# First attention of a four-layer kernel: another load order, four moves on the scalar queue, row transposes spread over the attention tiles

## Chip, cores, metric

One core of a Trainium2 chip. The metric is the device time of one execution in microseconds (us). A profile's span, first to last instruction, is about 1.8 us shorter than the time of the same execution. All times below are fast runs, or single profiled runs; those are called looks.

Names used below: TensorE (PE) does the matmuls; VectorE (DVE), ScalarE (ACT) and GpSimd (POOL) do the other arithmetic; transfers (DMA) are issued from the sync, scalar and gpsimd queues, and land when their semaphore shows them complete. An evacuation copies a matmul result out of PSUM, so that its accumulator is free again. A hole is time in which PE stands idle; a half clock is a stretch in which the trace's clock records grant PE 0.5.

## The reference, cut to what matters

Four layers, A B A B, on x of 2048 rows by 576. A is an attention of 32 heads of 18, each row looking at 8 rows at a distance of two. B is a gated layer. Row normalisation and residual additions, which matter here only as work between the layers, are cut.

```python
qkv = x @ wqkv                               # A: q, k, v of 576 each
logits = einsum('bhsd,bhswd->bhsw', q, kg) * scale   # 8 rows a head, masked
o = einsum('bhsw,bhswd->bhsd', softmax(logits), vg)
A = o.reshape(B, S, D) @ wo
# ...
z = gelu(einsum('bsd,df->bsf', x, w_in))     # B: its first half is gated by
                                             # a product over rows of the second
```

## The kernel before: the parts concerned

Everything below is in the first layer. Projections of q and k leave PSUM for staging tiles (`stg`, and `win2a`, lent for the last two head groups), and small transfers ("moves") carry 18-row pieces to their place in `QK`, from which the logits are computed. Eight moves belong to the last group, d = 4.

```python
def PG(d, qk, cc, dve, queues=(nc.sync, nc.gpsimd)):
    # ... five matmuls, evac() into stg; when a staging tile is full:
    for dst, src in moves:
        dma_rr[0] += 1
        self.dma(dst, src, eng=queues[dma_rr[0] % len(queues)])

def VW(t, hh, dve):                     # one v group: five matmuls into pv, then
    # ...
    evac(v_ext[...], pv[...], dve)      # VectorE if dve, else ScalarE

q2 = (nc.gpsimd, nc.sync, nc.gpsimd)
# ... loads, all on the sync queue
self.load_wv(nc.sync, 2)
x_load(x1[:, 0:4, :], 4, 4, nc.sync)    # x rows 512 on
self.load_wqk(nc.sync)                  # k, q, rest of k
# ... projections
PG(d, qk, cc, False, (nc.gpsimd, nc.sync) if d in (0, 4) else q2)
# ...
T_(12, 13, 14, 15)                      # row transposes of x rows 1536 on (sync queue)
for t in range(nvw0, nvw - (1 if li == 0 else 0)):
    for hh in range(2):
        VW(t, hh, li == 0)
```

The attention then runs in half tiles ("steps") of a table. Row transposes of the new x, which the gated layer needs, are put at steps:

```python
at(s + 2, LN_XN, i)                     # normalised row tile i; tiles 4 to 12 into stg
if i < NS - 1:
    at(max(s + 4, 24 + (5 * i) // 4) if li == 0 else s + 4, LN_T, i)   # its transpose
```

Every plain transposing transfer stands on the sync queue: the row transposes (`xnT`) and those of the attention output (`oT`). The gated layer's big tile `Z` is laid by the program over memory that the first attention used, `stg` included.

The softmax here doesn't subtract the row's maximum and nothing guards it: scores larger than these inputs give would overflow.

Of the kernel before, what the change touches and what calls it, by code (L numbers as in the profile page):

```python
# [19 lines left out]
D = 576  # L20
# [42 lines left out]
class K:  # L63
# [219 lines left out]
        nc.vector.memset(R["wv"][64:128, 4, :], 0.0)  # L283
        nc.vector.memset(R["wo"][64:128, 4, :], 0.0)

    def load_wqk(self, eng):

        R = self.right
        for c0, n, w0 in ((D, 512, D + 64), (0, D, 0), (D + 512, 64, D)):
            self.dma(R["wqk"][:, :, w0:w0 + n], self.A_wqkv[0:512, c0:c0 + n].rearrange("(c p) n -> p c n", p=P), eng=eng)  # L290
            self.dma(R["wqk4"][:64, w0:w0 + n], self.A_wqkv[512:576, c0:c0 + n], eng=eng)

# [29 lines left out]
    def layer_A(self, li):  # L322
        nc, tc, cfg = self.nc, self.tc, self.cfg
# [9 lines left out]
        NSTG, CBW = (3 if li == 0 else 4), 1024  # L333
        stgs = [main.tile([P, 2, CBW], bf16, name=f"stg{k_}") for k_ in range(NSTG)]
# [20 lines left out]
        def tdim(t):  # L355
            nq = min(QT, S - QT * t)
            return HALO + nq, nq
# [11 lines left out]
        def evac(out, in_, dve):  # L369
            if dve:  # L370
                nc.vector.tensor_copy(out=out, in_=in_)  # L371
            else:
                nc.scalar.copy(out=out, in_=in_)

        def VW(t, hh, dve):
            nk = tdim(t)[0]
            pv = self.PT_tile([P, 512], f32, "pv")
            for c in range(5):
                nc.tensor.matmul(pv[:nk, 0:288], lhsT=self.xnT[:, c, QT * t:QT * t + nk],  # L379
                                 rhs=wv_sb[:, c, hh * 288:(hh + 1) * 288], start=(c == 0), stop=(c == 4))  # L380
            evac(v_ext[:nk, t, 16 * hh:16 * hh + 16, 0:DH], pv[:nk, 0:288].rearrange("p (b d) -> p b d", d=DH), dve)
# [4 lines left out]
        def PG(d, qk, cc, dve, queues=(nc.sync, nc.gpsimd)):  # L386

            cb, gi = divmod(cc, CBW // 512)
            key = (d, cb)
            if key not in stg_tiles:  # L390
                if cb == 0 and d >= 3 and lent:
                    stg_tiles[key] = lent[d - 3]
                else:
                    stg_tiles[key] = stgs[stg_rr[0] % NSTG]
                    stg_rr[0] += 1
                stg_left[key] = (2 if d < 4 else 1) * (CBW // 512)
            stg = stg_tiles[key]
            pp = self.PT_tile([P, 512], f32, "pp")
            w0 = d * P + (640 if qk else 0)
            for c in range(5):  # L400
                w = wqk[:, c, w0:w0 + P] if c < 4 else wqk4[:, w0:w0 + P]
                nc.tensor.matmul(pp[:, :], lhsT=w, rhs=self.xnT[:, c, PADL + cc * 512:PADL + (cc + 1) * 512],  # L402
                                 start=(c == 0), stop=(c == 4))
            evac(stg[:, qk, gi * 512:(gi + 1) * 512], pp[:, :], dve)
            stg_left[key] -= 1
            if stg_left[key] == 0:
                stg_tiles.pop(key)
                cs = slice(PADL + cb * CBW, PADL + (cb + 1) * CBW)
                moves = []
                for h in range(d * P // DH, H):  # L410
                    a, b = max(h * DH, d * P), min((h + 1) * DH, (d + 1) * P)
                    if a >= b:
                        break
                    g, rg = divmod(h, 4)
                    q0, s0, n = 32 * rg + a - h * DH, a - d * P, b - a
                    if d < 4:
                        moves.append((QK[q0:q0 + n, :, g, cs], stg[s0:s0 + n, :, :]))
                    else:
                        for a_ in range(2):
                            moves.append((QK[q0:q0 + n, a_, g, cs], stg[64 * a_ + s0:64 * a_ + s0 + n, 0, :]))  # L420
# [3 lines that stand above are left out]
# [81 lines left out]
        def LN_XN(i):  # L505
            mv, rstd, nmr = tails[i].pop("ln")
            xn = None
            if li == 0 and 4 <= i < 4 + 3 * NSTG:
                k_, m = divmod(i - 4, 3)
                xn = stgs[(2 + k_) % NSTG][:].rearrange("p a b -> p (a b)")[:, 640 * m:640 * (m + 1)]  # L510
            tails[i]["xn"] = self.ln_xn(tails[i]["x"], P, mv, rstd, nmr, eng="pool", xn=xn)

        def LN_T(i):
# [2 lines left out]
        q2 = (nc.gpsimd, nc.sync, nc.gpsimd)  # L516


        if li == 0:
# [3 lines left out]
            def x_load(xg, i0, n, eng):  # L523
                self.dma(xg, self.A_x[i0 * P:(i0 + n) * P, :].rearrange("(i p) d -> p i d", p=P), eng=eng)
                for k_ in range(n):
                    xts[i0 + k_] = xg[:, k_, :]
# [3 lines left out]
            x_load(x0[:, 1:2, :], 1, 1, nc.scalar)  # L530
            x_load(x0[:, 2:4, :], 2, 2, nc.sync)
            self.load_wv(nc.sync, 2)
            x_load(x1[:, 0:4, :], 4, 4, nc.sync)
            self.load_wqk(nc.sync)
            x_load(spare, 8, 4, nc.sync)
            exp_table()
            self.zero_right()
# [12 lines left out]
            def S_(*tiles):  # L550
                for i in tiles:
                    st = sb.tile([P, 2, nc.vector.BN_STATS_DIM], f32, name="ln_st", tag="ln_st", bufs=3)
                    for s in range(2):
                        nc.vector.bn_stats(out=st[:, s, :], in_=xts[i][:, s * 288:(s + 1) * 288])
                    nc.vector.bn_aggr(out=mvs[:, i, :], in_=st[:])

            def R_(i0, n):
                rs = rstds[:, i0:i0 + n]
                nc.vector.tensor_scalar_add(out=rs, in0=mvs[:, i0:i0 + n, 1], scalar1=EPS)
                nc.gpsimd.tensor_tensor(out=rs, in0=rs, in1=self.neg_half[:, 0:1].to_broadcast([P, n]), op=ALU.pow)  # L560
# [29 lines left out]
            VW(0, 0, False)  # L590
            VW(0, 1, False)
            VW(1, 0, False)
            S_(3)
            R_(2, 2)
            rows[1]()
# [2 lines left out]
            A_(2, 3)  # L598
            T_pe(2)
            T_pe(3)  # L600
            VW(1, 1, False)
            x_load(sb.tile([P, 4, D], bf16, name="x_in3", tag="x_in", bufs=2)[:], 12, 4, nc.sync)
            S_(4, 5)
            R_(4, 2)
# [18 lines left out]
            order = [(d, 0) for d in range(4)] + [(d, 1) for d in range(4)] + [(4, 0), (4, 1)]  # L623
            for k_, (d, cc) in enumerate(order):
                for qk in ((1, 0) if d < 4 else (0,)):
                    PG(d, qk, cc, False, (nc.gpsimd, nc.sync) if d in (0, 4) else q2)
                if k_ == 3:
                    VW(3, 0, False)
                    VW(3, 1, False)
                if k_ == 5:  # L630
                    R_(12, 4)
                    A_(12, 13, 14, 15)
            T_(12, 13, 14, 15)
            nvw0, nvw = 4, 9
        else:
# [12 lines left out]
            nvw0, nvw = 0, 4  # L648
        for t in range(nvw0, nvw - (1 if li == 0 else 0)):
            for hh in range(2):  # L650
                VW(t, hh, li == 0)

        pieces = []

# [8 lines left out]
        def at(s, f, *a):  # L663
            table.setdefault(s, []).append((f, a))
# [6 lines left out]
        for t in range(nvw, NT):  # L671
            for hh in range(2):
                if li == 0 and t == nvw:
                    at(13 * hh, VW, t, hh, True)
                else:
                    at(2 * t - 2 + hh, VW, t, hh, 2 * t - 2 + hh >= PG_END and hh == 0)
        for i in range(NS):
            t = -(-(i + 1) * P // QT) - 1
            s = 2 * t + (6 if li == 0 and t < 10 else 5 if t < NT - 5 else 4 if t < NT - 3 else 3)
            at(s - 5, XO, i)  # L680
            at(s, WO, i, 0)
            at(s + 1, WO, i, 1)
            at(s + 1, LN_STATS, i)
            at(s + 2, LN_XN, i)
            at(s + 2, XST, i)
            if i < NS - 1:
                at(max(s + 4, 24 + (5 * i) // 4) if li == 0 else s + 4, LN_T, i)
        if li == 0:
            at(0, self.load_wo, nc.sync)
            for f in reversed(self.load_win2a(nc.gpsimd)):  # L690
                at(0, f)
        at(PG_END + 2, alloc_win2b)
        for k_ in range(6):
            at(PG_END + 2 + 2 * k_, win2b_piece, k_)
# [9 lines left out]
        if li == 0:  # L704
            VW(nvw - 1, 0, False)
            VW(nvw - 1, 1, False)
        for s in range(NST):
            if s + 1 < NST:
                L_mm(s + 1)
                EXP(s + 1)  # L710
            PV(s)
            for f, a in table.pop(s, []):
                f(*a)
# [339 lines left out]
```

## Time and profile before

| | |
|---|---|
| median of 3 runs | 1192.48 us (1191.74 to 1193.84) |
| span and mean granted clock of the profiled run | 1190.8 us, 0.998 |
| TensorE (PE) busy | 99% of the span |
| first logits; end of the attention's last output projection | 41.31 us; 135.31 us |

PE is the bound; only its holes, and stretches in which its clock is halved, can be won or added. The prediction shows the page's first lines and the waits. Two more views matter for what follows. First PE's timeline of the kernel before (start, length in us, line, operation, tiles, count, and in brackets the idle time before with what ended it):

```profile
34.05 5.16 PE L379 MATMUL pv<-wv_sb,xnT 128*128 128x288 bf16 x40
39.05 2.32 PE L402 MATMUL pp<-xnT,wqk_sb 128*128 128x512 bf16 x10
41.31 0.40 PE L437 MATMUL L_ps<-QK 32*128 32x112 bf16 x16
```

No bracket: eight v groups run on end, then two projections, then the first logits. Now the sync queue in the same view:

```profile
28.38 7.74 SPq L77 DMA_DIRECT2D QK<-stg  x9
...
41.93 5.20 SPq L249 DMA_TRANSPOSE xnT<-ln_xn  x4
```

Nine and seven moves are issued without a break (7.74 and 5.61 us, 0.8 us each), and then the four transposes of x rows 1536 on, which landed by 50.02 us. The attention loop's first projection needs them.

### The profile page before, as it was taken

To read this page: it belongs to the slowest core of one execution; us is meant where nothing else is said; L and a number is where in the kernel's file an instruction comes from. 1 tells how busy PE (TensorE), PEld (TensorE's weight loads), DVE (VectorE), ACT (ScalarE), POOL (GpSimd) and SP (SyncE) were. 2 spreads that over 40 slices of the span, in tenths; PEclk is the share of its full clock that TensorE was granted. 3 is DMA by queue.
4 is the path that set the end of the run, shared out by engine and by line. 5 is a ranking of instruction groups with operands and counts; after the bars stand their busy time and mean duration, and the time that the engine had idled before them with its cause. 6 is when DMAs were issued, how large, how long until landed. Compare 5 with 4: busy or idle time off the path is not lost.

```text
span 1190.8 us, 20761 instructions
## 1 busy us (share of the span) xinstructions
PE 1180.2 (99%) x8554; PEld 620.6 (52%) x8554; DVE 547.4 (46%) x1206; ACT 376.6 (32%) x593; POOL 281.5 (24%) x383
## 2 busy tenths in 40 slices
PE   8999999999999999999999999999999999999998
PEld 5567544444444444457755775444444444444677
DVE  8688587333233233245556786753233233233311
ACT  5578677210110110202156786760110110111000
POOL 4768685000000000001153877530000000000000
PEclk9999999999999999999999999999999999999999
DMA  8989992000000000049645999900000000000332
GB/s 195 200 163 199 181 224 65 23 4 9 12 12 12 12 1 11 12 139 291 169 98 117 203 227 196 202 14 9 12 12 1 12 12 12 12 1 28 125 105 73
DMA packets 178104, 101.21 MB, mean 85 GB/s; under 512 B 134336, under 2 KB 159360, under 8 KB 178009
## 3 DMA queue, kind: packets, MB, share of 16 engines
q1 hardware_dynamic: 165144, 78.13, 30.6%
q0 software_dynamic: 6512, 16.00, 5.4%
q10 hardware_dynamic: 6352, 5.75, 1.6%
q8 instruction: 67, 1.10, 0.4%
q14 instruction: 29, 0.23, 0.1%
HBM read 42.39 MB, written 16.53 MB: 49 GB/s over the span
## 4 chain that ended last, share of the span: by engine, by line
PE 94%; DMA 3%; POOL 1%; ACT 0%; issue 0%; SPq 0%; DVE 0%; ACTq 0%; DVEq 0%
PE pg L887 42%; PE pz L869 12%; PE po L941 12%; PE pz L791 11%; PE pp L402 5%; PE pw L494 3%; PE O_ps L457 3%; PE pv L379 3%; PE L_ps L437 2%; DMA oT<-o_t 2%; PE pzs L791 1%; DMA QK<-win2a 1%; POOL QK L77 1%; DMA wqk_sb<-in_A_wqkv_dram 1%; ACT P_sb L446 0%
## 5 line engine op out<-in xcount | busy, mean ns | idle before, releaser
L887 PE MATMUL pg<-Wq,Z 128*128 128x512 bf16 x2304 | 502.8, 379 | 0.0
L887 PEld LDWEIGHTS <-Z 128*128 128x128 bf16 x2304 | 225.3, 98 | 272.0
L891 DVE TENSOR_TENSOR g_tmp<-pg,ln_xn 128x512 f32<-128x512 f32 x144 | 99.6, 692 | 429.2 <-PE pg L887 429.2
L881 ACT ACTIVATE z1T<-pz 128x1024 bf16<-128x1024 f32 x72 | 73.7, 1024 | 513.8 <-PE pz L869 513.6
L77 POOL DMA_DIRECT2D wout<-in_B_w_out_dram x4 | 4.3, 1064 | 604.6 <-PE pg L887 604.6
L941 PE MATMUL po<-wout,Z 128*128 128x288 bf16 x1152 | 141.4, 286 | 0.0
L446 ACT ACTIVATE P_sb<-L_ps 128x896 bf16<-128x896 f32 (+1 forms) x152 | 126.7, 887 | 41.2 <-PE L_ps L437 40.6
L869 PE MATMUL pz<-xnT,w 128*128 128x512 bf16 (+1 forms) x640 | 136.0, 380 | 0.0
L941 PEld LDWEIGHTS <-Z 128*128 128x128 bf16 x1152 | 112.7, 98 | 28.8
L791 PEld LDWEIGHTS <-xnT 128*128 128x128 bf16 (+1 forms) x800 | 66.2, 97 | 81.0 <-issue 23.7
L791 PE MATMUL pz<-win2a,xnT 128*128 128x512 bf16 x384 | 104.8, 380 | 0.0
L892 DVE TENSOR_TENSOR Z<-g_tmp,z1T 128x512 bf16<-128x512 f32 x144 | 99.6, 692 | 9.7
L869 PEld LDWEIGHTS <-w 128*128 128x128 bf16 (+1 forms) x640 | 51.1, 97 | 80.0 <-issue 27.1
L402 PE MATMUL pp<-xnT,wqk_sb 128*128 128x512 bf16 x360 | 83.8, 382 | 0.5 <-DMA wqk_sb<-in_A_wqkv_dram 0.5
L805 ACT ACTIVATE zp<-pz 128x1024 bf16<-128x1024 f32 x64 | 65.5, 1024 | 36.6 <-PE pz L791 32.8
L951 DVE TENSOR_TENSOR x_new<-po,xo 128x288 f32<-128x288 f32 (+1 forms) x64 | 28.8, 455 | 87.6 <-PE po L941 83.5
L791 PE MATMUL pz<-win2b,xnT 128*128 128x512 bf16 (+1 forms) x256 | 65.7, 380 | 0.0
L807 DVE CUSTOM_DVE_ANT_0 Z<-zp 128x1536 bf16<-128x1536 bf16 x32 | 56.6, 1769 | 13.1 <-ACT zp L805 13.0
L77 POOL DMA_DIRECT2D QK<-stg x81 | 50.7, 631 | 36.3 <-DVE stg L371 21.0
L379 PE MATMUL pv<-wv_sb,xnT 128*128 128x288 bf16 (+1 forms) x380 | 55.8, 285 | 0.0
L242 POOL TENSOR_SCALAR ln_xn<-x_new,ln_mv,ln_rstd 128x576 bf16<-128x576 f32 x23 | 52.8, 2294 | 2.0
L402 PEld LDWEIGHTS <-wqk_sb 128*128 128x128 bf16 x360 | 33.2, 98 | 37.2 <-DMA wqk_sb<-in_A_wqkv_dram 1.0
(114 smaller groups left out, 916.9 us busy)
## 6 DMA issues: line engine op xcount, KB each, us to landing
xres<-x_new SPq DMA_DIRECT2D x48, 288.0 KB
xo<-xres SPq DMA_DIRECT2D x32, 288.0 KB
wout<-in_B_w_out_dram POOLq DMA_DIRECT2D x4, 1296.0 KB, 8.5
xo<-xres SPq DMA_DIRECT2D x8, 576.0 KB
w<-in_B_w_in_dram SPq DMA_DIRECT2D x16, 256.0 KB
QK<-stg POOLq DMA_DIRECT2D x53, 72.0 KB, 4.4
QK<-stg SPq DMA_DIRECT2D x41, 72.0 KB
xo<-in_A_x_dram SPq DMA_DIRECT2D x8, 288.0 KB
```

Of the source, the lines that this page charges most:

```text
L77: return eng.dma_start(out=out, in_=in_)
L379: nc.tensor.matmul(pv[:nk, 0:288], lhsT=self.xnT[:, c, QT * t:QT * t + nk], rhs=wv_sb[:, c, hh * 288:(hh + 1) * 288], start=(c == 0), stop ...
L402: nc.tensor.matmul(pp[:, :], lhsT=w, rhs=self.xnT[:, c, PADL + cc * 512:PADL + (cc + 1) * 512], start=(c == 0), stop=(c == 4))
L446: nc.scalar.activation(out=P_bufs[(2 * s + jp) % 4][:nk, :, :, 0:nq], in_=Lv[:nk, :, :, 0:nq], func=ACT.Exp, scale=scale)
L791: nc.tensor.matmul(pzvs[ci][:, sub * 512:sub * 512 + w], lhsT=self.xnT[r0:r1, c, PADL + i * P:PADL + (i + 1) * P], rhs=win2(c)[r0:r1, c0 + ...
L805: nc.scalar.activation(out=zp[:, c0:c0 + cn], in_=pzvs[ci][:, 0:cn], func=ACT.Gelu_apprx_tanh, accum_out=sums[:, ci:ci + 1])
L869: nc.tensor.matmul(pz1s[q // 2][:, q % 2, :], lhsT=w1[r0:r1, c, sub * P:(sub + 1) * P], rhs=self.xnT[r0:r1, c, PADL + q * 512:PADL + (q + ...
L881: nc.scalar.activation(out=z1T[:, q2 * 512:(q2 + 2) * 512], in_=pz1s[q2 // 2][:, :, :].rearrange("p a b -> p (a b)"), func=ACT.Gelu_apprx_ ...
L887: nc.tensor.matmul(pg[:, :], lhsT=Z[:, jj, i, sub * P:(sub + 1) * P], rhs=Wq[q][:, i, :], start=(i == 0), stop=(i == NS - 1))
L891: nc.vector.tensor_tensor(out=tmp[:], in0=pg[:, :], in1=bsp[:, qs], op=ALU.add)
L892: nc.vector.tensor_tensor(out=uT(jj)[:, sub, qs], in0=tmp[:], in1=z1Ts[jj, sub][:, qs], op=ALU.mult)
L941: nc.tensor.matmul(acc[hh], lhsT=uT(j // 2)[:, j % 2, i * P:(i + 1) * P], rhs=wouts[j // NJH][:, j % NJH, hh * 288:(hh + 1) * 288], start= ...
```

## The change

Its intent: q weights sooner; the gpsimd queue, whose last moves landed late, relieved by the scalar queue, with VectorE relieved of four v evacuations; and the sync queue free for output transposes.

```diff
-            x_load(x1[:, 0:4, :], 4, 4, nc.sync)
-            self.load_wqk(nc.sync)
+            self.load_wqk(nc.sync, ("k", "q0"))      # q0: the first 256 columns of q
+            x_load(x1[:, 0:4, :], 4, 4, nc.sync)
+            self.load_wqk(nc.sync, ("q1", "k1"))
...
-                    PG(d, qk, cc, False, (nc.gpsimd, nc.sync) if d in (0, 4) else q2)
+                    PG(d, qk, cc, False, (nc.gpsimd, nc.sync) if d == 0 else q2 if d < 4 else (nc.scalar, nc.sync))
...
-                VW(t, hh, li == 0)
+                VW(t, hh, li == 0 and t > 5)         # v tiles 4 and 5 now on ScalarE
...
-                at(max(s + 4, 24 + (5 * i) // 4) if li == 0 else s + 4, LN_T, i)
+                at(s + 4 if li > 0 or i > 12 else 21 + 2 * i if i < 7 else 35 + (i - 7) // 2, LN_T, i)
...
+            VW(nvw, 0, False)                        # taken out of step 13, ahead of the loop
```

Cut: one v group earlier in the prologue, another staging tile for the first normalised rows, and the order of six later weight loads.

More of the change, by code (lines that the diff above doesn't have):

```diff
@@ L284, in zero_right, with load_wqk @@
         nc.vector.memset(R["wo"][64:128, 4, :], 0.0)
-    def load_wqk(self, eng):
+    def load_wqk(self, eng, names=("k", "q", "k1")):
         R = self.right
-        for c0, n, w0 in ((D, 512, D + 64), (0, D, 0), (D + 512, 64, D)):
+        parts = dict(k=(D, 512, D + 64), q=(0, D, 0), q0=(0, 256, 0), q1=(256, D - 256, 256), k1=(D + 512, 64, D))
+        for c0, n, w0 in (parts[k_] for k_ in names):
             self.dma(R["wqk"][:, :, w0:w0 + n], self.A_wqkv[0:512, c0:c0 + n].rearrange("(c p) n -> p c n", p=P), eng=eng)
@@ L509, in LN_XN @@
                 k_, m = divmod(i - 4, 3)
-                xn = stgs[(2 + k_) % NSTG][:].rearrange("p a b -> p (a b)")[:, 640 * m:640 * (m + 1)]
+                xn = stgs[(1 + k_) % NSTG][:].rearrange("p a b -> p (a b)")[:, 640 * m:640 * (m + 1)]
             tails[i]["xn"] = self.ln_xn(tails[i]["x"], P, mv, rstd, nmr, eng="pool", xn=xn)
@@ L592, in layer_A @@
             VW(1, 0, False)
+            VW(1, 1, False)
             S_(3)
@@ L600, in layer_A @@
             T_pe(3)
-            VW(1, 1, False)
             x_load(sb.tile([P, 4, D], bf16, name="x_in3", tag="x_in", bufs=2)[:], 12, 4, nc.sync)
@@ L673, in layer_A @@
                 if li == 0 and t == nvw:
-                    at(13 * hh, VW, t, hh, True)
+                    if hh == 1:
+                        at(0, VW, t, hh, True)
                 else:
@@ L686, in layer_A @@
             if i < NS - 1:
-                at(max(s + 4, 24 + (5 * i) // 4) if li == 0 else s + 4, LN_T, i)
+                at(s + 4 if li > 0 or i > 12 else 21 + 2 * i if i < 7 else 35 + (i - 7) // 2, LN_T, i)
         if li == 0:
             at(0, self.load_wo, nc.sync)
-            for f in reversed(self.load_win2a(nc.gpsimd)):
-                at(0, f)
+            w2l = self.load_win2a(nc.gpsimd)
+            for k_ in (3, 5, 4, 2, 1, 0):
+                at(0, w2l[k_])
         at(PG_END + 2, alloc_win2b)
```

## The prediction

> **What bounds the kernel now.** I read the page first, for the engine that has no time to spare, then the waits of that engine inside the first attention (the change touches nothing else), then the timelines of the engines that end those waits.
>
> ```profile
> PE 1180.2 (99%) x8554; PEld 620.6 (52%) x8554; DVE 547.4 (46%) x1206; ACT 376.6 (32%) x593; POOL 281.5 (24%) x383
> PE 94%; DMA 3%; POOL 1%; ACT 0%; issue 0%; SPq 0%; DVE 0%; ACTq 0%; DVEq 0%
> ```
>
> The matmul engine is busy 99% of the span and carries 94% of the chain. What a reordering can win is the holes of PE, at most some 10 us of 1191, and only those before about 134 us, where the first attention ends (the gated layer's matmuls, line 791, take over there). So faster or slower by 2% (24 us) is out of reach; the question is one of single microseconds. The waits of PE in 0 to 52 and 50 to 140 us:
>
> ```profile
> PE pt L574 <- DVE ln_xn L567: 1.2, 2, 0.8
> PE L_ps L437 <- DMA QK<-win2a: 0.7, 1, 0.7
> PE pp L402 <- DMA wqk_sb<-in_A_wqkv_dram: 0.5, 1, 0.5
> ...
> PE pw L494 <- DMA oT<-o_t: 1.8, 2, 1.2
> PE L_ps L437 <- ACT P_sb L446: 0.9, 3, 0.3
> ```
>
> Each part of the change has one of them as its target: the q weights (0.5), the last head moves (0.7), the row transposes that hold up those of the attention output (1.8). A fourth cost is no wait. Timeline of PE, and a window with granted clock (ninth column):
>
> ```profile
> 50.90 2.29 PE L402 MATMUL pp<-xnT,wqk_sb 128*128 128x512 bf16 x5
> 54.08 1.24 PE L402 MATMUL pp<-xnT,wqk_sb 128*128 128x512 bf16 x5
> ...
> 51.00:52.00 1.00, 1.00 (x5) 0.31 (x3) 0.71 (x2) 1.00 (x2) 0.05 (x1) 0.50 1.06 395
> ```
>
> The same five matmuls take 2.29 instead of 1.24 us: right after the wait for the head moves (at 48.2 to 48.9 us) the clock is halved. The trace's clock records have it at 0.5 from 50.52 to 53.93 us, and not again before the last instructions.
>
> **What the Trainium skill says.** "TensorE: Matmul & The Clock Gate", Part 1, says that the clock falls to half after an idle window of about 3.4 us and returns after a busy one. The trace agrees in the window (3.41 us at half clock), but PE was not idle in the window before: it had a 0.7 us hole and small matmuls. So low activity suffices here, and a wait that lies among 128x512 matmuls need not cost a clock window. "DMA: Bandwidth & Descriptors", Issuing engines are not separate DMA queues, says that transfers from the scalar, sync and gpsimd queues share the same 16 engines and that several issuers only save sequencer time. The trace agrees: the head moves land 3 to 5.5 us after issue on both queues, later the more are under way. The same page, DMA Transpose (X-bar), allows plain transposes only from the hardware queues and forbids two transposing streams at once; so they all stand in line on the sync queue, as the trace shows.
>
> **Part 1, x after the first q weights: removes a small wait, makes a larger one.** All these loads stand in one backlogged queue, so their order is their order of landing. From the semaphore times in the trace: wv 7.7 us, x rows 512 on 10.8, k 12.5 to 12.7, q 14.4, the last k part 15.1 to 15.4, x rows 1024 on 16.6. PE needs q at 13.76 (end of the first k group) and starts it at 14.47. With k and 256 columns of q ahead of x, q is there by about 12 us. The order of PE also puts the fourth v group before the second pair of transposes; the third v tile then waits for its evacuation, so I put the first projection at 12.85 instead of 12.68. Eight of 1.08 us and two v groups (1.22 us) bring PE to rows 512 on at 22.7, not 23.26: 0.56 us gained.
>
> But those rows land later, by k (12.7 - 10.8 = 1.9) and 256/576 of q (0.45 x 2.15 = 1.0): 13.7 us. VectorE's order is unchanged:
>
> ```profile
> 10.84 0.82 DVE L554 BATCH_NORM_STATS2 ln_st<-x_in 128x6 f32<-128x288 bf16 x2 [0.36 <-DMA x_in<-in_A_x_dram]
> 16.66 0.82 DVE L554 BATCH_NORM_STATS2 ln_st<-oT 128x6 f32<-128x288 bf16 x2 [0.83 <-DMA oT<-in_A_x_dram]
> 17.64 0.85 DVE L567 TENSOR_SCALAR ln_xn<-x_in,lnx_mv,lnx_rstd 128x576 bf16<-128x576 bf16 x2
> ```
>
> Start 10.84 becomes 13.74, the wait of 0.83 at 16.66 absorbs some, and normalising tiles 6 and 7 moves from 17.64 to 19.7. Their transposes move by 2.07 us; the last landed at 22.06 (semaphore time), so now about 24.1. PE, which had 1.2 us in hand, waits 1.4 us at 22.7 and goes on at 24.15, **0.9 us later than before**. VectorE, the window-row fill and the sync queue are 2 us late from here on.
>
> **Part 2, last head moves on the scalar queue, four v evacuations on ScalarE.** Four of the eight last moves leave GpSimd, where they were issued from 42.0 to 46.0 us, partly waiting for free semaphores; the last landed at 48.8 and ended PE's wait. On ScalarE they go right after the last projection's evacuation (34.25 + 0.59 + 0.9 = 35.8 us). The sync queue's price for such moves:
>
> ```profile
> 36.22 5.61 SPq L77 DMA_DIRECT2D QK<-win2a  x7
> ```
>
> 0.8 us each; the only early issue on ScalarE took 0.42. At 0.5 to 0.75 ScalarE is free at 37.8 to 38.8. Only then does it evacuate v tiles 4 and 5. PE has four small accumulators: it computes four v groups from 35.0 to 37.4 and then waits for the first evacuation, at 38.2 to 39.2: **0.8 to 1.7 us lost**, take 1.2. Then come four v groups, six projections, the first logits and three v groups (one from the loop has been put here): about 2.45 + 6.5 + 0.4 + 1.84 us, so PE reaches the second logits at about 49.8, where the hole began at 47.3 before. The sync queue is 2 us late and must also wait for semaphores that it shares with ScalarE, so its last moves land at 48 to 50. The wait goes to about zero, with 1.15 us of PE time (start to end of these 16 matmuls 1.75 us, 0.6 without the hole), and with the halved clock another 1.05 (2.29 - 1.24).
>
> At the end of the first projection in the loop (53.1 us before) I get 53.9, with one v group (0.61) more already done. Late transposes of x rows 1536 on (issued from about 45 instead of 41.9) could add up to 1 us just there; I put in 0.3.
>
> **Part 3, the v group taken out of step 13.** It has left a place where PE has time anyway: from 78.4 to 87.9 us five steps take 1.89 us each, and two steps between waits for ScalarE's exponentials take 1.845. Of 0.61 us only about 0.2 come back.
>
> **Part 4, row transposes spread, one an attention tile.** This is the clear gain. Sync queue before:
>
> ```profile
> 119.68 1.25 SPq L249 DMA_TRANSPOSE xnT<-stg  x1
> 121.02 1.78 SPq L469 DMA_TRANSPOSE oT<-o_t  x1
> 122.90 1.23 SPq L249 DMA_TRANSPOSE xnT<-stg  x1
> 124.18 0.57 SPq L77 DMA_DIRECT2D xres<-x_new  x1
> 124.84 1.23 SPq L249 DMA_TRANSPOSE xnT<-stg  x1
> 126.17 0.53 SPq L77 DMA_DIRECT2D xo<-in_A_x_dram  x1
> 126.80 1.19 SPq L469 DMA_TRANSPOSE oT<-o_t  x1
> ```
>
> The output tile issued at 121.0 was ready at 117.6, that at 126.8 at 122.3 (end of its probability-times-v group plus 1.2 us for the division). They landed 4.2 and 4.6 us later, at 125.18 and 131.38, and PE waited 0.59 and 1.23 us. After the change a tile of 4.3 us holds one output transpose, one row transpose, a store and half a load, 1.3 + 1.3 + 0.6 + 0.3 = 3.5 us; the queue keeps up, the outputs land 3 to 4 us earlier, and both waits go: **1.8 us gained**. Seven row transposes now come behind the last output transpose; the next layer needs tile i only at 133.5 + 4.6 i us, so they cost nothing.
>
> **Sum.** Head: 53.9 + 0.3 - 53.1 = +1.1; step 13: -0.2; tail: -1.8. That is -0.9 us. The two added waits of the head are the least sure terms and can be smaller (the loads overlap at their ends, ScalarE may issue in 0.4 us); with half of them gone it is -2.2. Between the two: **-1.8 us, 1190.7 us**.
>
> **Rivals.** (1) The head is a clean gain: rows 512 on in time, head moves in time, no halved clock. For it: PE had 1.2 us in hand at 23.26, and the v evacuations moved off VectorE look as if its lateness had been provided for. Against it: VectorE is a serial chain and starts on those rows 2.9 us later. Then -2.5 in the head, 1188.0 us. (2) The waits pile up: ScalarE blocked over 3 us by its issues, moves or transposes of rows 1536 on late at the logits or the loop's first projections, the halved clock elsewhere. For it: the sync queue 2 us late, semaphores shared between two issuers. Then head +3, 1193.5 us. (3) The tail's waits are hidden anyway or replaced by ScalarE's copy of the last output tiles. Against it: two long v-free stretches show PE idle for exactly these transposes; if so the tail gives only 0.6 and the time is 1192.
>
> **Range and chances.** Runs of the kernel before lie between 1191.7 and 1193.8, so noise alone is 1 us; the rivals span 1188 to 1193.5. Range 1188.2 to 1193.2. Within 2%: 0.99.
>
> **What would show it.** In the changed profile: no wait for the q weights near 14 us; statistics of rows 512 on starting near 13.7; a PE hole of 1 to 1.5 us before 24 us that a row transpose ends; a hole near 38 us that ScalarE's v evacuation ends; no hole at the second logits and full clock at 50 to 54 us; output transposes issued within 1.5 us of the division and no wait for them after 120 us. If the statistics start before 12 us, part 1 is wrong; if there is no hole near 38 us, part 2; if output transposes still end waits, part 4.

## The result, and the profile after

The changed kernel took **1194.65 us** (median of 6 runs, 1192.91 to 1198.08), the kernel before 1192.11 on the same chip. The ratio is 1.0026, with a 95% interval of 1.0007 to 1.0044: within 2%, but slower, and outside the predicted range. (A ratio here is the mean time of one kernel's fast runs over that of the other's of the same rounds, so not quite the ratio of the quoted medians.)

PE is still busy 99%. Its waits up to 52 us in the profiled run of the changed kernel (us in total, times, longest):

```profile
PE pv L380 <- ACT v_ext L374: 2.9, 1, 2.9
...
PE pp L403 <- DMA xnT<-ln_xn: 0.6, 1, 0.6
```

The hole foreseen at 0.8 to 1.7 us is 2.9; that at rows 512 on is 0.6. The wait for the q weights and that at the second logits are gone. The timelines of PE and of ScalarE show the hole and its cause:

```profile
34.24 2.61 PE L380 MATMUL pv<-wv_sb,xnT 128*128 128x288 bf16 x20
39.79 4.07 PE L380 MATMUL pv<-wv_sb,xnT 128*128 128x288 bf16 x20 [2.94 <-ACT v_ext L374]
43.66 2.58 PE L403 MATMUL pp<-xnT,wqk_sb 128*128 128x512 bf16 x10
46.17 0.40 PE L438 MATMUL L_ps<-QK 32*128 32x112 bf16 x16
```

```profile
34.44 0.59 ACT L374 CAST win2a<-pp 128x512 bf16<-128x512 f32 x1 [0.49 <-PE pp L403]
35.06 4.24 ACTq L77 DMA_DIRECT2D QK<-win2a  x4
39.34 1.31 ACT L374 CAST v_ext<-pv 128x288 bf16<-128x288 f32 x4 [4.31 <-DMA QK<-win2a]
```

The four issues hold ScalarE for 4.24 us (1.44, 0.75, 0.72 and 1.20), and its v evacuations come behind them. The releaser named in the bracket, a landing move, is not what they waited for: they start 0.04 us after the last issue ends. A window of the changed kernel, with the granted clock in the column after the five engines:

```profile
41.00:42.00 1.00, 1.00 (x6) 0.63 (x5) 0.52 (x2) 0.00 (x0) 0.59 (x1) 0.50 0.82 115
```

The clock records have 0.5 from 40.75 to 44.17 us. So the same twenty v matmuls take 4.07 us behind the hole and 2.61 ahead of it. First logits: 46.17 us instead of 41.31.

The sync queue, its waits from 28 to 52 us and its timeline:

```profile
SPq L77 <- DMA QK<-stg: 2.8, 2, 1.5
...
SPq L77 <- DMA QK<-win2a: 0.4, 1, 0.4
```

```profile
40.24 5.92 SPq L77 DMA_DIRECT2D QK<-win2a  x7
46.26 5.24 SPq L249 DMA_TRANSPOSE xnT<-ln_xn  x4
```

Before, this queue waited for no landing. Now it waits 3.2 us for landings (3.3 counted as gaps between issues), and the last row transposes are issued 4.3 us later and land at 52.9. PE does not notice, since it comes to them only at 55.69: the loss at ScalarE hides this one. Why a queue waits for a *landing* is in the trace's semaphore records, of which this is an extract (not a profile view):

```
issue at  queue   semaphore  last user of it, landed at
37.92     sync    104        sync move of 33.26,   37.906
40.24     sync    105        sync move of 34.09,   40.173
43.09     sync    108        scalar move of 36.54, 43.032
```

All transfers of the sync and the scalar queue take turns at eight completion semaphores; those of gpsimd have eight of their own. A transfer is issued only when the previous user of its semaphore has landed, here within 0.07 us of it. Four scalar moves among those of the sync queue use up four turns. The Trainium skill's "DMA: Bandwidth & Descriptors", section "Why a DMA increments its semaphore by 16 and not by 1", gives the reason to wait: a shared semaphore can pass before the earlier transfer has wholly landed, so it wants one semaphore for each slot in flight. The trace agrees with that practice; the section gives no cost for the wait.

At the tail the waits for output transposes after 120 us are gone, as predicted: last output projection at 136.82 us, 1.51 behind the kernel before, having been 2.90 behind at 128. But the gated layer gives part of it back. Its first write to `Z` on VectorE, before and after:

```profile
139.72 1.76 DVE L807 CUSTOM_DVE_ANT_0 Z<-zp 128x1536 bf16<-128x1536 bf16 x1 [2.69 <-ACT zp L805]
```

```profile
141.82 1.76 DVE L812 CUSTOM_DVE_ANT_0 Z<-zp 128x1536 bf16<-128x1536 bf16 x1 [3.28 <-DMA xnT<-stg]
...
155.34 0.81 PE L796 MATMUL pz<-win2a,xnT 128*128 128x512 bf16 x3 [1.03 <-ACT zp L810]
```

Before, the data released it. After, a row transpose reading `stg`, landed at 141.65, did, since `Z` lies over `stg`. PE pays 1.03 us for it. From there on both kernels run alike but for small differences in the second attention.

### The profile page after: what moved, and what is told of

The parts are those of the page before. It is cut to its first block, busy times and chain, and to the rows that moved or that the text cites. A ratio compares the mean times of both kernels' runs of the same rounds, so it can differ in the third digit from the quotient of the medians.

```text
span 1194.0 us, 20760 instructions
## 1 busy us (share of the span) xinstructions
PE 1180.6 (99%) x8554; PEld 621.6 (52%) x8554; DVE 545.7 (46%) x1201; ACT 377.5 (32%) x598; POOL 279.2 (23%) x379
## 4 chain that ended last, share of the span: by engine, by line
PE 93%; POOL 1%; ACT 1%; DVE 1%; DMA 1%; issue 1%; SPq 1%; ACTq 0%; POOLq 0%; DVEq 0%
PE pg L892 42%; PE pz L874 12%; PE po L946 12%; PE pz L796 10%; PE pp L403 6%; PE pv L380 3%; PE pw L495 3%; PE O_ps L458 3%; PE L_ps L438 2%; PE pzs L796 1%; ACT P_sb L447 1%; POOL ln_xn L242 1%; DMA x_in<-in_A_x_dram 1%; SPq L77 1%; DMA xnT<-ln_xn 0%
## 5 line engine op out<-in xcount | busy, mean ns | idle before, releaser
L447 ACT ACTIVATE P_sb<-L_ps 128x896 bf16<-128x896 f32 (+1 forms) x152 | 126.3, 887 | 38.4 <-PE L_ps L438 37.8
```

Source lines behind the costliest of these rows:

```text
L447: nc.scalar.activation(out=P_bufs[(2 * s + jp) % 4][:nk, :, :, 0:nq], in_=Lv[:nk, :, :, 0:nq], func=ACT.Exp, scale=scale)
```

## The experiments

Sixteen kernels ran, all with correct results. The first twelve had five rounds each against the kernel before; the last four were looks.

### Undo one part at a time

**a_moves_pool**: the changed kernel with the last moves back.

```diff
-(nc.gpsimd, nc.sync) if d == 0 else q2 if d < 4 else (nc.scalar, nc.sync)
+(nc.gpsimd, nc.sync) if d in (0, 4) else q2
```

> The changed kernel with the last head moves issued from GpSimd and sync again, all else as changed. Theory S (the scalar queue is the loss: its four issues took 4.24 us, the v evacuations stood behind them, PE lost 2.9 us at 37 us and then 1.4 us to a halved clock): the hole before 39.8 us shrinks from 2.9 to under 0.3 us, no halved clock at 41 us, and the time falls by 2.3 to 4.4 us against the changed kernel (to about 1190.3 to 1192.4), less so if the hole and halved clock at the second logits (1.2 and 1.1 us in the kernel before) come back. Rival R (the row transposes and what they do to the gated layer are the loss): the time stays within 1 us of the changed kernel. Rival X (x rows 512 on arriving late is the loss): the same, within 1 us.

1192.03 us, ratio 1.0007 (0.9994 to 1.0021). PE's timeline at the same place:

```profile
34.13 5.06 PE L380 MATMUL pv<-wv_sb,xnT 128*128 128x288 bf16 x40
39.03 2.32 PE L403 MATMUL pp<-xnT,wqk_sb 128*128 128x512 bf16 x10
```

Hole, half clock and sync-queue waits for landings are gone. Its interval overlaps that of the changed kernel, so the times alone do not part these two; but of the versions below that keep the moves on the scalar queue in the same rounds, two lie clear above it (a_v_dve, a_rows_old) and the third touches it (a_x_old). The loss belongs to the scalar queue's moves; not yet to one mechanism of them.

**a_v_dve**: the four v evacuations back on VectorE, the moves still on the scalar queue.

```diff
-VW(t, hh, li == 0 and t > 5)
+VW(t, hh, li == 0)
```

> The changed kernel with the four v evacuations given back to VectorE, the moves staying on the scalar queue. Theory S in its narrow form (the issues themselves cost nothing, only the evacuations behind them do): VectorE is free at 37.4 us, so PE's hole is about 0.6 us instead of 2.9, no halved clock at 41 us, time down by 3 to 4 us, to about 1191. If the loss were the moves landing late or the two issuers in each other's way, the hole would move to the first or second logits (46 to 53 us) and the time would stay within 1 us of the changed kernel.

1195.64 us, ratio 1.0042 (1.0025 to 1.0059). The hole shrank to 1.1 us, but this took its place (PE's waits; and the sync queue's):

```profile
PE pp L403 <- DMA xnT<-ln_xn: 4.7, 1, 4.7
```

```profile
SPq L77 <- DMA QK<-stg: 1.8, 2, 1.3
```

So the theory that only the evacuations behind the issues cost fell. With PE on time, the late row transposes are what it meets, and the clock halved in that wait. The last of them was issued at 50.0 and landed at 56.7, so it was late at both ends.

**a_rows_old**: the old steps of the row transposes. **a_x_old**: x ahead of all k and q weights again.

```diff
-at(s + 4 if li > 0 or i > 12 else 21 + 2 * i if i < 7 else 35 + (i - 7) // 2, LN_T, i)   # a_rows_old
+at(max(s + 4, 24 + (5 * i) // 4) if li == 0 else s + 4, LN_T, i)
-self.load_wqk(nc.sync, ("k", "q0")); x_load(x1[:, 0:4, :], 4, 4, nc.sync); self.load_wqk(nc.sync, ("q1", "k1"))
+x_load(x1[:, 0:4, :], 4, 4, nc.sync); self.load_wqk(nc.sync)                             # a_x_old
```

> The changed kernel with the row transposes at the steps of the kernel before, all else as changed. Theory S+B (spreading wins 1.8 us at the end of the attention and gives back 1.2 us in the gated layer, whose first write into the shared buffer waits for the last row transpose): the two waits of the output projection after 120 us (0.6 and 1.2 us) come back, the wait of 1.0 us near 155 us goes, the time changes by less than 1 us. Rival R (the spreading is the loss): the time falls by over 1.5 us.

> The changed kernel with x rows 512 on loaded ahead of k and q again. Theory S: the load order was worth +0.2 us at 23.3 us of PE time (0.6 won, 0.6 waited, 0.2 from the moved v group) and leaves the hole at 37 us, since that is set by ScalarE: time within 1 us of the changed kernel. Rival X: VectorE, fill and moves 1.25 us earlier lets everything behind it start earlier, time down by over 1.5 us.

1195.04 us, 1.0037 (1.0023 to 1.0051), and 1194.26 us, 1.0031 (1.0019 to 1.0043). PE's hole stayed in both, first in a_rows_old, then in a_x_old:

```profile
PE pv L380 <- ACT v_ext L374: 2.4, 1, 2.4
```

```profile
PE pv L380 <- ACT v_ext L374: 2.6, 1, 2.6
```

Neither part is the loss. In a_rows_old the gated layer's wait is gone and an output wait of 0.9 is back.

### Do one part alone

**b_moves_act**: the kernel before with the moves on the scalar queue, v evacuations on VectorE. **b_rows_new**: the kernel before with the new steps of the row transposes.

```diff
-(nc.gpsimd, nc.sync) if d in (0, 4) else q2                                              # b_moves_act
+(nc.gpsimd, nc.sync) if d == 0 else q2 if d < 4 else (nc.scalar, nc.sync)
-at(max(s + 4, 24 + (5 * i) // 4) if li == 0 else s + 4, LN_T, i)                         # b_rows_new
+at(s + 4 if li > 0 or i > 12 else 21 + 2 * i if i < 7 else 35 + (i - 7) // 2, LN_T, i)
```

> Kernel before with one part of the change alone: the eight moves of the last head group alternate between the scalar and the sync queue instead of the gpsimd and the sync queue. v evacuations of this stretch stay on VectorE, as in the kernel before. Theory S (issuing from the scalar queue is the loss, whoever does the v evacuations): median 1193.0 to 1195.0, and the last row transposes before the attention land 1 us or more later than the 50.0 of the kernel before. Rival C (only the combination with v evacuations on ScalarE costs): 1190 to 1192 and no hole of TensorE over 1.2 us between 36 and 41 us. Rival R (the loss is chance of the clock): within 1190 to 1192, and runs at a mean clock of 1.0 at 1189 to 1190.5.

> Kernel before with the new steps of the row transposes alone. The prediction gave this part -1.8 us: two output projections waiting 0.59 and 1.23 us for output transposes. Theory G (it is given back at the gated layer, whose first tile lies over the staging buffers that the last row transposes read): output-projection waits under 0.4 us in all, but the gated layer's first DVE write waits 2 us or more for a row transpose that lands at 140 or later, and the median is within 0.8 us of the kernel before. Rival (the prediction's step): 1188.0 to 1189.0.

b_moves_act: **1197.72 us, 1.0047** (1.0024 to 1.0070), worse than the whole change. No hole ahead of the first logits, which start at 41.31 as before; the sync queue waits 3.2 us for landings, and PE's timeline has

```profile
54.61 0.58 PE L402 MATMUL pp<-xnT,wqk_sb 128*128 128x512 bf16 x1 [3.42 <-DMA xnT<-ln_xn]
```

with a half clock of 6.83 us from 52.89. This is the second loss by itself, without ScalarE: late sync issues, late row transposes. The last one was issued at 48.8 us, against 45.1 to 45.9 in four profiles of the kernel before (three of them are the looks below), and took 5.7 us to land, against 4.1 to 5.5; so most of its lateness is late issue. One thing I overlooked: with four moves fewer, GpSimd issues its first weight loads of the gated layer sooner, here at 41.4 us (44.1 to 46.0 before), and in a_v_dve and a_swap (below) the last row transpose took 6.7 and 8.5 us to land with such loads in flight. Whether transfers crowding one another add to the loss was not tested.

b_rows_new: 1191.02 us, 0.9994 (0.9977 to 1.0011). Its output waits are gone, and the first write to `Z` waits:

```profile
137.32 1.76 DVE L807 CUSTOM_DVE_ANT_0 Z<-zp 128x1536 bf16<-128x1536 bf16 x1 [3.72 <-DMA xnT<-stg]
...
149.96 0.81 PE L791 MATMUL pz<-win2a,xnT 128*128 128x512 bf16 x3 [0.60 <-ACT zp L805]
```

The releasing row transpose landed at 136.8, not at 140 or later as expected. The mechanism at the gated layer thus comes from the new steps alone; in this kernel it costs 0.76 us from the last output projection to one input projection in the middle of the gated layer (the one that ends at 391.67 us in the kernel before: 257.12 against 256.36 in every profile of the kernel before). From the last probability-times-v to that mark its profile has 261.30 us; the four profiles of the kernel before have 260.69 to 263.48, so one profile settles no gain.

**b_rows_early**: the same spreading, four steps earlier.

```diff
-at(max(s + 4, 24 + (5 * i) // 4) if li == 0 else s + 4, LN_T, i)
+at(s + 4 if li > 0 or i > 12 else 17 + 2 * i if i < 9 else (34, 35, 36, 36)[i - 9], LN_T, i)
```

> Kernel before with the row transposes spread over the attention tiles as the change does, but four steps earlier, so that fewer stand behind the last output transpose. If theory G is right, the last transpose that reads the staging buffers lands by 138.0, the gated layer waits 0.5 us or less, and the 1.8 us of the output-projection waits are kept: median 1188.3 to 1189.5, ratio about 0.9985. Rival (spreading itself moves the waits elsewhere, or gains nothing because the waits for output transposes stay): 1190 to 1191.5.

1191.05 us, 0.9998 (0.9982 to 1.0014). As foreseen in the trace, the output waits are gone, the first write to `Z` is again released by its data,

```profile
137.48 1.76 DVE L807 CUSTOM_DVE_ANT_0 Z<-zp 128x1536 bf16<-128x1536 bf16 x1 [2.69 <-ACT zp L805]
```

and the stretch after it takes 256.36 us. The time does not show the expected gain: the median lies in the rival's range, and the interval is as wide as the gain.

### Keep the scalar queue and take its two prices away

**a_moves_late**: the four scalar issues behind ScalarE's v evacuations. **a_swap**: the last moves on scalar and gpsimd, so that sync gives up its four. **a_swap_late**: both.

```diff
-self.dma(dst, src, eng=eng)
+if eng is nc.scalar: late_moves.append((dst, src))     # a_moves_late: issued after v tile 5
+else: self.dma(dst, src, eng=eng)
-(nc.scalar, nc.sync)
+(nc.scalar, nc.gpsimd)                                 # a_swap
```

> Changed kernel, with the four moves of the last head group that go on the scalar queue issued behind the four v evacuations of ScalarE instead of ahead of them. Same queue, same bytes. Theory S1 (the issues hold ScalarE while TensorE needs its evacuations; the queue itself is no loss): the hole of 2.9 us ahead of 39.8 falls under 0.7, the clock keeps its full rate there, median 1191.0 to 1192.5. Rival S2 (moves on the scalar queue land too late or crowd the transfers whenever they are issued): median 1194 or more, with waits on DMA QK or on the last xnT transposes of 1 us or more.

> Changed kernel, with the eight moves of the last head group alternating between the scalar and the gpsimd queue, so that the sync queue gives up its four in place of the gpsimd queue. The scalar issues still stand ahead of the v evacuations of ScalarE. Theory L (the transfers of the scalar and the sync queue take turns at the same eight completion semaphores, and four more of them make issues of the sync queue wait for landings, 3.2 to 4 us in all before the last row transposes in every run with these moves on the scalar queue, 0 in the others): the sync queue waits for no DMA QK, its last row transposes issue by 41.5 and land by 50.5, and the median is 1190.5 to 1192.5 although the TensorE hole of 2 to 3 us ahead of 39 us stays. Rival S1 (what costs is ScalarE held by the issues): 1194 or more.

> As the run before it, and the scalar issues behind the v evacuations as well. Theory L: no hole over 0.7 us, no wait of the sync queue for DMA QK, last row transposes land by 50.5, median 1189.5 to 1191.0; with the two loss causes apart, the step from the run before is that of ScalarE alone, 0.5 to 1.5 us. Rival (moving the scalar queue's traffic at all costs, by contention of the transfers): 1193 or more.

| kernel | PE hole at the v groups | sync waits for landings | last row transpose lands | PE waits for it | ratio (95%) |
|---|---|---|---|---|---|
| changed | 2.9 | 3.3 | 52.9 | 0 | 1.0026 (1.0007 to 1.0044) |
| a_moves_late | 0 | 3.2 | 54.5 | 2.2 | 1.0033 (1.0019 to 1.0047) |
| a_swap | 3.3 | 3.4 | 55.6 | 0 | 1.0032 (1.0011 to 1.0052) |
| a_swap_late | 0 | 2.4 | 51.9 | 0.2 | 1.0016 (0.9996 to 1.0037) |
| a_moves_pool | 0 | 0 | 51.7 | 0 | 1.0007 (0.9994 to 1.0021) |

(Times in us, from one profile each; waits for landings are the gaps between issues that end within 0.12 us of the landing on the same semaphore.)

Both single expectations fell, and in all three runs the median came out in the range of the rival (1195.83, 1195.87 and 1194.27 us). a_moves_late took ScalarE's hold away and gained nothing: PE now met the late transposes,

```profile
54.61 0.58 PE L404 MATMUL pp<-xnT,wqk_sb 128*128 128x512 bf16 x1 [2.18 <-DMA xnT<-ln_xn]
```

beside 1.5 us for moves at the second logits. In a_swap my idea that giving up four sync moves would end the waits was wrong: the four scalar moves still take their four turns ahead of later sync transfers, so the waits stayed at 3.4 us, and the hole stayed too. Only with the issues moved *and* the sync queue's list shortened does a kernel with scalar moves come near; 1194.27 us, above the kernel before of its rounds by 0.16%, not resolved from it, nor from a_moves_late. It still has 2.4 us of stalls, so its rival, that transfers crowd one another, is not excluded. Its profile is of its slowest run. PE waits in it for an output transpose (issued at 80.2, landed at 87.1),

```profile
87.16 1.38 PE L500 MATMUL pw<-wo_sb,oT 128*128 128x288 bf16 x5 [1.87 <-DMA oT<-o_t]
```

and a half clock of 6.83 us begins in that wait, at 86.5; a second, of 3.41 us, begins at 697.5 in the second attention, 0.3 us after a like wait of 2.2 us.

### Versions meant to be best

**a_swap_late_early** adds the earlier row transposes to a_swap_late; **a_pool_early** adds them to a_moves_pool.

```diff
-at(s + 4 if li > 0 or i > 12 else 21 + 2 * i if i < 7 else 35 + (i - 7) // 2, LN_T, i)
+at(s + 4 if li > 0 or i > 12 else 17 + 2 * i if i < 9 else (34, 35, 36, 36)[i - 9], LN_T, i)
```

> As a_swap_late with the row transposes four steps earlier, so that the gated layer's first tile does not wait for the last of them. If the gated layer still waited in a_swap_late, this is 0.5 to 1.0 faster; expected 1188.5 to 1190.5 and below the kernel before of the same rounds by 0.5 us or more. Rival (the gain is drowned in the chance of the half-clock windows): ratio to the kernel before within 0.999 to 1.001.

> Changed kernel with the last head's moves back on the gpsimd and sync queues (none on the scalar queue) and the row transposes four steps earlier: both causes found so far taken out, the x order, the moved v group and the spreading kept. If the two causes are the whole loss, the sync queue waits for no DMA QK, output-projection waits are under 0.4 us, the gated layer waits 0.5 us or less, and the ratio to the kernel before is 0.9975 to 0.9995 (1.8 us of output-projection waits less the chance of the half-clock windows). Rival (the two parts kept are worth nothing on the clock of the whole program): 0.9995 to 1.001.

1192.93 us, 1.0002 (0.9985 to 1.0019), and 1191.95 us, 1.0010 (0.9992 to 1.0029). In both traces the targeted waits in the first attention and at the gated layer are small or gone, though a_swap_late_early still has 1.9 us of sync waits for landings. a_pool_early's profile loses 1.1 us again to an output transpose in the *second* attention. Neither beats the kernel before. The rival stood: the parts kept are worth nothing that these rounds resolve.

### Looks at the unchanged kernels

What remained odd: versions without the two losses should have beaten the kernel before by the waits seen in its profile. So I profiled it three times more, and the changed kernel once.

> The kernel before, unchanged, profiled once more. Theory V (the waits that the prediction counted as fixed costs of the kernel before vary from run to run): in a run of mean clock 1.0, 1189 to 1190.5 us, the second logits wait may stay but without a half-clock window, and the two output-projection waits (0.59 and 1.23 us in the first profile) come to under 0.9 us together. Rival (they are fixed, and only the half-clock window comes and goes): 1.6 to 2.0 us of output-projection waits in every profile, and a clean run ends 1.0 to 1.3 us earlier than the profiled one, no more.

> A second look at the kernel before, unchanged; as c_before1. If the profile falls with a half-clock window near 50 us again, the second-logits wait is 0.5 us or more ahead of it.

> A third look at the kernel before, unchanged; the same expectations as for c_before1.

> The changed kernel, unchanged, profiled once more. Fixed, if the explanation is right: sync-queue waits for landings of QK moves of 2.5 to 4 us in all before the last row transposes, the TensorE hole of 2 to 3.5 us behind ScalarE's issues, the last row transposes landing at 52 or later, and the gated layer's first tile waiting for the last row transpose. By chance: where a half-clock window falls. In a clean run 1192.5 to 1194.

1191.55, 1190.31, 1191.77 and 1194.26 us. From the traces, the time between six marks in PE's work (the fourth is the input projection named at b_rows_new; the last is PE's last matmul):

| stretch of PE (us) | before | c_before1 | c_before2 | c_before3 | after | c_after1 |
|---|---|---|---|---|---|---|
| start to first logits | 41.31 | 40.66 | 40.60 | 40.60 | 46.17 | 45.58 |
| to the last probability-times-v | 88.43 | 88.88 | 86.70 | 86.76 | 86.47 | 86.48 |
| to the last output projection | 5.57 | 4.33 | 5.72 | 7.12 | 4.18 | 4.18 |
| to an input projection in the middle of the gated layer | 256.36 | 256.36 | 256.36 | 256.36 | 257.56 | 256.84 |
| to the second attention's last probability-times-v | 325.82 | 326.21 | 325.82 | 325.82 | 326.12 | 325.96 |
| to PE's last matmul | 470.28 | 470.28 | 470.28 | 470.28 | 470.28 | 470.28 |

Adding up, the mean of the two after is 3.3 us above the mean of the four before: +5.1 to the first logits, -1.2 and -1.5 in the next two stretches, +0.8 at the gated layer, +0.1 in the second attention.

The table also shows that the profile I predicted from was the slowest of the four. Its wait for the q weights is in none of the others, where the q projections start at 13.78 to 13.88 us, as in the changed kernel (13.89 and 13.98). The half clock near 50 us is in two of four: none in c_before2, and in c_before3 it came at 129.8 instead and lengthened the third stretch to 7.12. The second-logits wait is 2.0 us in c_before1 and in c_before2

```profile
47.77 0.22 PE L437 MATMUL L_ps<-QK 32*128 32x112 bf16 x1 [0.31 <-DMA QK<-win2a]
```

The output waits come to 1.8, 0, 1.6 and 1.4 us. So theory V holds in that these costs vary from run to run, but not in the form I gave it: in the clean run (no half clock before its last instructions), c_before2, the output waits were 1.6 us, where under 0.9 was expected. The rival fell too, since c_before1 has none and the clean run ended 2.3 us earlier than the first profile, not 1.0 to 1.3.

In c_after1 the expected fixed losses came again in PE's timeline:

```profile
39.20 3.87 PE L380 MATMUL pv<-wv_sb,xnT 128*128 128x288 bf16 x20 [3.04 <-ACT v_ext L374]
42.87 2.78 PE L403 MATMUL pp<-xnT,wqk_sb 128*128 128x512 bf16 x10
```

Against c_before2 the first logits are 4.98 us later: 3.04 of hole, 1.42 in the v groups (3.87 against 2.45 for twenty at full clock, as four groups follow another four there) and 0.46 in the two projections (2.78 against 2.32) at half clock, and 0.10 before them: 5.02. At `Z` the view names ScalarE's data as the releaser in this run; but the row transpose landed at 140.52 and the write began at 140.69, the same 0.17 us later as in the first profile (141.65, 141.82), and the stretch is 0.48 us longer than before. The transpose is likely, and not shown, to have released it here too.

## Why the prediction was wrong

**Part 1** was right in kind and too large at both ends. The 0.56 us to be won at the q weights is a chance of one profile. Rows 512 on landed at 13.01 us (12.17 in c_after1), not 13.7: the 2.9 us that I added from differences of landing times came to 2.2. PE waited 0.6 us instead of 1.4, and in c_after1 not at all. a_x_old shows no gain from undoing the order.

**Part 2 is the step that failed.** "At 0.5 to 0.75 ScalarE is free at 37.8 to 38.8 ... take 1.2": four issues took 4.24 us, not 2 to 3, and the hole was 2.9 to 3.0. Then the sentence that a wait among larger matmuls "need not cost a clock window": in both profiles of the changed kernel it did, at 1.9 us for the 4.98 of c_after1. Third, the credit of 1.15 and 1.05 us for the second-logits wait and the half clock was taken as a fixed cost of the kernel before; it is there in some runs only. The sync queue's waits for shared semaphores were named in the text, but sized at a late landing only. They were 3.3 us and are a second loss that lies beside the first: b_moves_act has it alone, and a_moves_late shows it in place of the hole. How much of that second loss is stalled issue and how much slower landing stays open. Head: +1.1 predicted. Against the four profiles of before, it is 5.1 to the first logits and 3.9 by the last probability-times-v. Rival 2, "the waits pile up", 1193.5 us, was the right picture and still too small.

Three slips in its working are too small to explain the miss. From 37.4 to 39.2 us is 1.8, not 1.7. The head moves landed 2.9 to 6.1 us after issue, not 3 to 5.5. And from its own terms the first projection of the loop ends at 49.8 + (53.1 - 47.3) - 1.15 - 1.05 = 53.4, not 53.9; the sum would then have been -1.4 instead of -0.9.

**Part 3** was not tested alone. The second stretch is 0.2 to 0.3 us shorter than in c_before2 and c_before3, which agrees with -0.2 but mixes other waits.

**Part 4**: the 1.8 us of output waits went, in both profiles, and for the reason given: those two output transposes were issued 0.7 and 0.4 us after their division in the changed kernel, 2.7 and 3.8 before (the prediction's tiles ready at 117.6 and 122.3 were ready at 118.3 and 123.0). "so they cost nothing" failed: I looked at when the gated layer reads row tile i and not at what its first write lies over. b_rows_new shows the wait with this part alone, b_rows_early its absence when the transposes come four steps sooner. It costs 0.5 to 1.2 us of the gain.

What stays open: whether spreading the row transposes is worth anything in the median. The traces say up to 1.5 us, and two timed versions, 0.9994 and 0.9998, cannot tell that from nothing. Also which of the runs get a half-clock window. The Trainium skill's "TensorE: Matmul & The Clock Gate", Part 1, calls the window free-running and its effect run-variable; the four profiles of one program, with half clocks at 50.5, 51.4, nowhere and 129.8 us, agree.

## What to carry to other kernels

Before moving transfers to a compute engine's queue, count what the engine has to do behind the issues, and which completion semaphores the new transfers will share: four issues here cost that engine 4.2 us and another queue 3.3 us of waits. Two losses of like size lying beside each other make each single repair look useless, so try both together before dropping a theory. And a wait of a microsecond seen in one profile is a sample: look at the unchanged kernel several times before crediting its removal, and when work is put later, check what the next stage's first *write* lies over.

## What the Trainium skill lacked or had wrong

- "DMA: Bandwidth & Descriptors", Why a DMA increments its semaphore by 16 and not by 1: lacks the cost of a limited set of semaphores. In this program sync and scalar transfers take turns at eight, and the sync queue stalled 1.39, 1.54 and 0.42 us until earlier users had landed; no stall with the moves on gpsimd, which has its own eight.
- "DMA: Bandwidth & Descriptors", Issuing engines are not separate DMA queues: the saving of sequencer time has a price that this section does not size (tables elsewhere on the page give sequencer cycles for earlier generations, not what an engine's own work loses). A move (of at most 18 rows) held ScalarE 0.72 to 1.44 us at issue (4.24 us for four); on the sync queue such a move took about 0.8 us and on gpsimd about 0.6.
- "DMA: Bandwidth & Descriptors", DMA Transpose (X-bar): this section has no duration for a queue of small ones. Here one mostly held the sync queue 1.2 to 1.3 us and the last landed 2.6 to 8.5 us after its issue.
- "TensorE: Matmul & The Clock Gate", Part 1: gives in its table of states about 3.4 us of idleness before the clock falls; short idles, which it names later as another case, get no length. Here it fell with less: 0.96 us after a hole of 2.94 us had ended, and 1.7 us after one of 0.69; a hole of 2.4 us in a_rows_old was followed by none. The length of the slow stretch, 3.41 or 6.83 us, agrees.
